# Fewer weight tiles converted during attention, at half the pace, and fewer low-urgency dummy matmuls

## The chip, the cores and the metric

The kernel runs on one core of a Trainium2 chip. The metric is the device time of one execution in microseconds (us). Three runs of the kernel before took 681.79, 682.04 and 682.61 us.

## The reference

The inputs are queries, keys and values (2 batches, 8 heads, 768 positions, head dimension 64, float32), two integers, and five weight matrices in float64. What is computed, in short:

```python
# attention: scores with a slope per head, a local window and a few global keys
scores = q @ k.T / sqrt(64) - slope[h] * dist        # dist: distance, or n_local for a far global key
keep = (key < n_global) | ((rel >= 0) & (rel < n_local))
a = softmax(where(keep, scores, -1e9));  x = a @ v    # then reshaped to 1536 tokens x 512
# first feed-forward layer: h * tanh(softplus(h))
h = x @ w_in;  x = (h * tanh(log1p(exp(min(h, 20))))) @ w_out          # 512 -> 2048 -> 512
# second feed-forward layer: gated
g = x @ w_gate;  out = (g * sigmoid(g) * (x @ w_val)) @ w_out2         # 512 -> 1536 -> 512
```

## The kernel before, in words

The kernel writes its instruction order itself. It first enters every operation of the program in a planner (`Plan`), with the engines that may do it, an estimated cost, what it reads and writes, and a due time. The due time of a TensorE operation is the sum of the TensorE costs entered so far; that of any other operation is 7 us later, unless an operation that needs its result pulls it forward. Then `Plan.order` plays the program through: whenever an engine is free in that play, it takes the ready operation with the earliest due time, wherever in the program it was entered. An operation is ready when its inputs are there and its buffers have come free, in the order in which they were asked for. The resulting order per engine is fixed when the program is built; on the chip each engine works through its list and waits where an input is late.

**Attention** goes over 12 tiles of 128 tokens, each in two steps of four heads (24 steps, variable `s` of the loop). A step has: transposes of queries and keys for the next tile (L440), the score matmuls (L469), the bias and row minimum on DVE (L488), the exponentials on ACT (L322, tile `e`), transposes of the exponentials (L530) and their copies out of the banks (tile `et`). Once per tile the inverse row sums are spread (L501 to L511) and multiplied with the product with the values (L551, L559); the result is split in a high and a low part in tile `x`.

**Feed-forward.** The tokens stand in three chunks of 512. A job is one chunk and one block of 128 hidden columns: 12 matmuls for the hidden block (L362, three passes over high and low parts), the activation on ACT, DVE and POOL, and 12 matmuls for the output. For the first layer jobs go in pairs. A pass is a half of the blocks (8) for one chunk; the output sums over the pass stay in four banks and are copied out where two passes meet. The first pair needs four weight tiles, the first pass sixteen.

**Weight tiles.** A weight tile (a unit, 68 of them) is loaded as float64 (tile `raw`, 512 KB, 2 buffers), turned into float32 by one ACT pass (L393) and four DVE passes (L876 to L879, tile `cv`, 3 buffers), and split into a high part (L345 on ACT or L342 on POOL) and a low part (L353, on POOL or DVE). It ends in one of the 13 buffers `wa`, or, once attention has given up its memory, one of 15 buffers `wb`. The loop over the steps calls `units_to(n)`, which enters conversions until n are entered. The calls behind the loop, between the jobs, enter the others.

**Dummy matmuls.** `warm_up` enters 6 + `LATE` matmuls on a zero tile (L585). The first 6 are due at once. The others are due last of all, so that TensorE takes one when nothing else is ready in the planner's play.

The matmuls of the feed-forward layers get their first banks when the score matmuls are done. The instruction lines in the profile can be lines of helpers (L322, L342, L345, L353, L362); the tile names tell them apart.

Of the kernel before, what the change touches and what calls it, by code (L numbers as in the profile page):

```python
# [212 lines left out]
def kernel(  # L213
# [25 lines left out]
    NWA = 13  # L239
    NWB = 15  # L240
    NST = 2
    WARM = 6
    LATE = 50
    EDGE = 104
    SPARE = 2500.0
    SCALE = -1.0 / float(D) ** 0.5
# [134 lines left out]
    def convert(u):  # L381
        key, (src, view) = units[u]
        raw = plan.buf(raw_p)
        w = plan.buf(cv_p)
        t = plan.buf(w_p)
        where[key] = t
        hi = lambda: raw.t[:, :, 1]
        lo = lambda: raw.t[:, :, 0]
        wf = lambda: w.t.bitcast(F32)
        R, W_ = [(raw, 0)], [(w, 0)]  # L390
        dma(lambda: nc.sync.dma_start(out=view(raw.t), in_=src), [], R, kb=512)
        steps = f64_steps(nc, lambda: w.t, lo, hi)
        op([("A", 520, lambda: nc.scalar.activation(out=wf(), in_=hi().bitcast(F32), func=AF.Abs))], R, W_)  # L393
        for i, fn in enumerate(steps):
            op([("V", (450, 500, 780, 840)[i], fn)], R + W_ if i > 1 else W_, W_)
        copy(lambda: t.t[:, 0], wf, W_, [(t, 0)], on="AG")
        arith(lambda: t.t[:, 1], wf, lambda: t.t[:, 0].bitcast(F32), ALU.subtract, W_ + [(t, 0)], [(t, 1)])
# [6 lines left out]
    def load(i, names="qk"):  # L404
        b, t = tiles[i]
        for nm, src in (("q", q), ("k", k), ("v", v)):
            if nm not in names:
                continue
            x = plan.buf(raw_in[nm])
            raws[nm, i] = x  # L410
            for hs in (slice(0, 4), slice(4, 8)) if i == 0 else (slice(0, H),):
                dma(lambda x=x, src=src, hs=hs: nc.sync.dma_start(
                    out=x.t[:, hs], in_=src[b, hs, t * P:(t + 1) * P, :].rearrange("h s d -> s h d")), [],
                    [(x, hf) for hf in range(hs.start // 4, hs.stop // 4)], kb=32 * (hs.stop - hs.start),
                    prio=-1e6 + hs.start + 9 * (nm == "v") if i == 0 else None)

    def load_previous(i):

        b, t = tiles[i]
        if t == 0:  # L420
            raws["u", i] = raws["v", i]
        elif t < NT - 1:
            x = raws["u", i] = plan.buf(raw_in["u"])
            for ks, k0, hk in ((slice(0, WG), 0, 0), (slice(WG, P), t * P + WG, 1)):
                dma(lambda ks=ks, k0=k0: nc.sync.dma_start(
                    out=x.t[ks], in_=v[b, :, k0:k0 + ks.stop - ks.start, :].rearrange("h s d -> s h d")), [],
                    [(x, hk)], kb=2 * (ks.stop - ks.start))

    def transp(i, hf):
        b, t = tiles[i]  # L430
        xk, xq = raws["k", i], raws["q", i]
        ps = plan.buf(t_p)
        c = t % 2
        prs = slice(2 * hf, 2 * hf + 2)

        def emit():
            for p in range(4):
                x = xq if p % 2 else xk
                h = 4 * hf + p // 2 * 2
                nc.tensor.transpose(ps.t[:, p * P:(p + 1) * P], x.t[:, h:h + 2, :].rearrange("s h d -> s (h d)"), ident)  # L440

        pe(emit, [(xk, hf), (xq, hf)], [(ps, 0)], 4, 128)
        copy(lambda: kq.t[:, prs, c:3:2 - c, :], lambda: ps.t.rearrange("p (a b s) -> p a b s", a=2, b=2), [(ps, 0)],
             [(kq, (c, hf)), (kq, (2, hf))], psum_in=True, on="AV")

    def move_k(i, hf):
        b, t = tiles[i]
        if t == NT - 1:
            return
        prs = slice(2 * hf, 2 * hf + 2)  # L450
        own = lambda: kq.t[:, prs, t % 2, 0:WG]
        g = lambda: kg.t[:, prs, :]
        if t == 0:
            copy(g, own, [(kq, (t % 2, hf))], [(kg, hf)], n=64, on="G")
        else:
            copy(own, g, [(kg, hf)], [(kq, (t % 2, hf))], n=64, on="G")

    def qk(s):
        i, hf = divmod(s, 2)
        b, t = tiles[i]  # L460
        nb = 1 if t == 0 else 2
        banks = scs[s] = [plan.buf(sc_p[0]), plan.buf(sc_p[1])]

        def emit():
            for p in range(2):
                pr = 2 * hf + p
                for j in range(2):
                    ro = slice(64 * j, 64 * j + 64)
                    nc.tensor.matmul(out=banks[j].t[:, p * 256:p * 256 + nb * P], lhsT=kq.t[ro, pr, 2, :],  # L469
                                     rhs=kq.t[ro, pr, 0:nb, :].rearrange("p b s -> p (b s)"), start=True, stop=True)  # L470

        pe(emit, [(kq, (c, hf)) for c in (2, 0, 1)[:nb + 1]], [(banks[0], 0), (banks[1], 0)], 8, 230, "RR")

    def softmax(s):
        i, hf = divmod(s, 2)
        b, t = tiles[i]
        n = P if t == 0 else 2 * P
        banks = scs.pop(s)
        e = ebs[s] = plan.buf(e_p)
        if hf == 0:  # L480
            sms[i] = plan.buf(sm_p)
        sm = sms[i]
        m = lambda u: mn.t[:, s * 4 + u:s * 4 + u + 1]
        for u in range(4):
            p, j = divmod(u, 2)
            h = 4 * hf + u
            bs, c0 = (bias0, 0) if t == 0 else (bias, (1 - t % 2) * P)
            dve(lambda u=u, p=p, j=j, h=h, bs=bs, c0=c0: nc.vector.tensor_tensor_reduce(  # L488
                out=e.t[:, u, 0:n], in0=banks[j].t[:, p * 256:p * 256 + n], in1=bs.t[:, h, c0:c0 + n], scale=SCALE,
                scalar=BIG, op0=ALU.add, op1=ALU.min, accum_out=m(u)),  # L490
                [(banks[j], 0), (bs, h)], [(e, u), (mn, s * 4 + u)], n=n + 8)
        for u in range(4):
            act(lambda u=u: e.t[:, u, 0:n], lambda u=u: e.t[:, u, 0:n], AF.Exp, [(mn, s * 4 + u)],
                [(e, u), (sm, 4 * hf + u)], scale=-1.0, bias_=lambda u=u: m(u),
                accum=lambda u=u: sm.t[:, 4 * hf + u:4 * hf + u + 1], n=n)
# [21 lines left out]
    def turn(s):  # L517

        nb = blocks(s)
        e = ebs.pop(s)  # L520
        ets[s] = []
        for p in range(2):
            ps = plan.buf(t_p)
            et = plan.buf(et_p)
            pv4 = lambda ps=ps: ps.t.rearrange("p (c j s) -> p c j s", c=2, j=2)

            def emit(p=p, pv4=pv4):
                for c in range(nb):
                    for j in range(2):
                        nc.tensor.transpose(pv4()[:, c, j, :], e.t[:, 2 * p + j, c * P:(c + 1) * P], ident)  # L530

            pe(emit, [(e, 2 * p), (e, 2 * p + 1)], [(ps, 0)], 2 * nb, 128)
            copy(lambda et=et: et.t[:, 0:nb], lambda pv4=pv4: pv4()[:, 0:nb], [(ps, 0)], [(et, 0)],
                 psum_in=True, n=256 * nb, on="AV")
            ets[s].append(et)
# [43 lines left out]
    def warm_up(first, later):  # L579
        src, ps = plan.buf(g_p), plan.buf(warm_p)  # L580
        t = lambda: src.t.rearrange("p a c -> p (a c)")
        op([("V", 600, lambda: nc.vector.memset(t()[:, 0:512].bitcast(F32), 0.0))], [], [(src, 0)], prio=-1e5)

        def emit():
            nc.tensor.matmul(out=ps.t, lhsT=t()[:, 0:P], rhs=t()[:, 0:512], start=True, stop=True)  # L585

        for i in range(first + later):
            op([("P", 216, emit)], [(src, 0)], [(ps, i)], prio=-1e5 if i < first else 1e6)
        plan.nominal = 0.0

    def setup():
        warm_up(WARM, LATE)
        load(0, "qk")
# [197 lines left out]
    def units_to(n):  # L791
        while n_units[0] < min(n, len(units), freed[0] + room[0]):
            convert(n_units[0])
            n_units[0] += 1

    NS = 2 * NTL
    for s in range(NS + 2):
        i, hf = divmod(s, 2)
        if s < NS:
            if hf == 0:  # L800
                load_previous(i)
                if i + 1 < NTL:
                    load(i + 1, "v")
            qk(s)
            softmax(s)
            move_k(i, hf)
            if i + 1 < NTL:
                transp(i + 1, hf)
            if hf == 1 and i + 2 < NTL:
                load(i + 2)  # L810
        if 0 <= s - 1 < NS:
            turn(s - 1)
            if s % 2 == 0:
                spread(s // 2 - 1)
                pv(s // 2 - 1)
        units_to(min(NWA, max(0, s - 3)))
        if s == NS:
            flag()
    def switch():
# [299 lines left out]
```

## Time and profile before

| | |
|---|---|
| median of three runs | 682.04 us |
| profiled execution | 681.4 us |
| its span in the profile | 679.6 us |
| granted TensorE clock, mean | 0.996 |
| instructions | 9295 |
| TensorE busy | 660.2 us |
| DVE, ACT, POOL busy | 385.0, 358.6, 273.3 us |

Times in rows are microseconds from the start of the span unless marked ns. PE is TensorE's matmul, PEld its weight load; DVE is VectorE, ACT ScalarE, POOL GpSimd, SP the engine that issues the loads and stores. In a group, "out<-in" names the tiles written and read. Busy time of an engine says that something ran on it, not that it was needed: a dummy matmul counts as busy.

### The profile page before, as it was taken

What the parts mean: (1) busy time and instruction counts of PE and PEld (TensorE: products, weight loads), DVE (VectorE), ACT (ScalarE), POOL (GpSimd) and SP (SyncE); (2) the same over time, 40 slices, a digit from 0 to 9 for tenths busy, and PEclk for the clock granted to TensorE, in tenths of its full rate; (3) what the DMA queues carried; (4) which work ended last, traced back from release to release, by engine and by line L of the source; (5) the groups of instructions that cost most, each with busy time, mean ns of one, the idle gap of its engine ahead of it and who ended that gap; (6) DMA issues with size and microseconds to landing.
All of it is one profiled execution on the core that took longest, in us unless ns stands there. A gap on an engine that the chain in (4) does not pass through costs nothing.

```text
span 679.6 us, 9295 instructions
## 1 busy us (share of the span) xinstructions
PE 660.2 (97%) x3369; PEld 539.4 (79%) x3369; DVE 385.0 (57%) x711; ACT 358.6 (53%) x653; POOL 273.3 (40%) x271
## 2 busy tenths in 40 slices
PE   8999999998998999999989999999999999999996
PEld 5877678887887888888868788888888888888884
DVE  6899978788658475773695798111761121312212
ACT  6999898878775787577758322211521211111110
POOL 3567653754445444563474373211531111111110
PEclk9999999999998999999999999999999999999999
DMA  8788851233334326122043124100300300300301
GB/s 201 187 203 212 216 134 63 92 111 125 98 103 127 110 74 217 62 94 94 31 124 123 63 72 145 62 1 1 123 32 0 124 1 0 124 0 1 125 0 66
DMA packets 80068, 63.58 MB, mean 94 GB/s; under 512 B 48272, under 2 KB 68752, under 8 KB 80016
## 3 DMA queue, kind: packets, MB, share of 16 engines
q1 hardware_dynamic: 80016, 62.93, 30.7%
q8 instruction: 28, 0.46, 0.3%
q14 instruction: 24, 0.20, 0.1%
HBM read 53.48 MB, written 9.44 MB: 93 GB/s over the span
## 4 chain that ended last, share of the span: by engine, by line
PE 72%; ACT 11%; DVE 9%; issue 4%; DMA 2%; POOL 1%; SPq 1%; DVEq 0%; ACTq 0%; POOLq 0%
PE bank L362 62%; PE bank L469 2%; PE bank L530 2%; PE bank L551 2%; ACT u L322 2%; DVE cv L879 2%; ACT e L322 1%; PE bank L585 1%; DVE cv L876 1%; ACT u L698 1%; DVE cv L878 1%; ACT L697 1%; DVE a L353 1%; PE bank L440 1%; ACT cv L393 1%
## 5 line engine op out<-in xcount | busy, mean ns | idle before, releaser
L353 POOL TENSOR_TENSOR g<-a,g 128x512 fp32r<-128x512 f32 x65 | 91.6, 1412 | 228.9 <-ACT g L345 227.8
L362 PE MATMUL bank<-x,wa 128*128 128x512 f32 x756 | 180.0, 390 | 0.0
L362 PEld LDWEIGHTS bank<-x,wa 128*128 128x128 f32 x756 | 141.6, 188 | 29.3
L362 PE MATMUL bank<-x,wb 128*128 128x512 f32 x684 | 162.0, 389 | 0.0
L362 PEld LDWEIGHTS bank<-x,wb 128*128 128x128 f32 x684 | 128.4, 188 | 26.6
L322 ACT ACTIVATE u<-bank 128x512 f32<-128x512 f32 x84 | 49.6, 591 | 119.9 <-PE bank L362 119.7
L716 DVE SCALAR_TENSOR_TENSOR a<-u,bank 128x512 f32<-128x512 f32 x36 | 24.7, 685 | 144.5 <-ACT u L322 144.5
L345 ACT ACTIVATE g<-a 128x512 fp32r<-128x512 f32 x66 | 41.1, 630 | 90.3 <-DVE a L718 78.6
L362 PE MATMUL bank<-g,wa 128*128 128x512 f32 x288 | 71.0, 397 | 3.8 <-DVE st L342 1.9
L362 PE MATMUL bank<-g,wb 128*128 128x512 f32 x288 | 69.1, 389 | 2.6 <-DVE st L577 2.6
L362 PE MATMUL bank<-wa,g 128*128 128x512 f32 x288 | 69.5, 389 | 1.2 <-DVE st L577 1.2
L362 PEld LDWEIGHTS bank<-g,wa 128*128 128x128 f32 x288 | 55.1, 192 | 16.2 <-ACT st L345 2.3
L876 DVE TENSOR_SCALAR cv<-cv 128x512 f32<-128x512 f32 x68 | 43.8, 648 | 41.7 <-ACT cv L393 41.4
L362 PEld LDWEIGHTS bank<-g,wb 128*128 128x128 f32 x288 | 53.9, 188 | 14.2 <-issue 3.0
L362 PEld LDWEIGHTS bank<-wa,g 128*128 128x128 f32 x288 | 54.0, 188 | 12.8 <-ACT cv L393 1.6
L879 DVE SCALAR_TENSOR_TENSOR cv<-raw,cv 128x512 int32<-128x512 int32 x68 | 61.6, 910 | 1.1
L878 DVE SCALAR_TENSOR_TENSOR cv<-raw,cv 128x512 int32<-128x512 int32 x68 | 59.2, 876 | 0.9
L353 POOL TENSOR_TENSOR wa<-cv,wa 128x512 fp32r<-128x512 f32 x32 | 44.5, 1390 | 32.2 <-ACT wa L345 29.8
L353 DVE TENSOR_TENSOR a<-bank,u 128x512 f32<-128x512 f32 x48 | 30.9, 685 | 42.1 <-ACT u L322 41.1
L393 ACT ACTIVATE cv<-raw 128x512 f32<-128x512 f32 x68 | 44.9, 666 | 16.7 <-DMA raw<-in_moe_w_gate_dram 7.5
L353 POOL TENSOR_TENSOR wb<-cv,wb 128x512 fp32r<-128x512 f32 x25 | 36.4, 1459 | 30.0 <-ACT wb L345 29.3
L322 ACT ACTIVATE e<-e,mn 128x256 f32<-128x256 f32 (+1 forms) x96 | 46.0, 487 | 1.7 <-DVE mn L488 1.7
(96 smaller groups left out, 790.8 us busy)
## 6 DMA issues: line engine op xcount, KB each, us to landing
raw<-in_moe_w_out_dram SPq DMA_DIRECT2D x28, 512.0 KB, 3.3
raw<-in_moe_w_in_dram SPq DMA_DIRECT2D x16, 512.0 KB, 3.9
raw<-in_moe_w_gate_dram SPq DMA_DIRECT2D x12, 512.0 KB, 3.5
raw<-in_moe_w_val_dram SPq DMA_DIRECT2D x12, 512.0 KB, 3.5
part<-st SPq DMA_DIRECT2D x12, 256.0 KB, 2.0
part<-sb SPq DMA_DIRECT2D x12, 256.0 KB, 2.2
st<-part SPq DMA_DIRECT2D x12, 256.0 KB, 2.7
sb<-part SPq DMA_DIRECT2D x12, 256.0 KB, 3.7
```

The lines of the kernel that those rows point to most:

```text
L322: nc.scalar.activation(out=o(), in_=i(), func=func, scale=scale, **args)
L345: lambda: nc.scalar.activation(out=o(), in_=i(), func=AF.Copy, scale=scale)),
L353: return lambda: eng.tensor_tensor(out=o(), in0=x(), in1=y(), op=alu)
L362: nc.tensor.matmul(out=o, lhsT=lhs(a), rhs=rhs(b), start=first and i == 0, stop=last and i == len(PASSES) - 1)
L393: op([("A", 520, lambda: nc.scalar.activation(out=wf(), in_=hi().bitcast(F32), func=AF.Abs))], R, W_)
L469: nc.tensor.matmul(out=banks[j].t[:, p * 256:p * 256 + nb * P], lhsT=kq.t[ro, pr, 2, :], rhs=kq.t[ro, pr, 0:nb, :].rearrange("p b s -> p ( ...
L530: nc.tensor.transpose(pv4()[:, c, j, :], e.t[:, 2 * p + j, c * P:(c + 1) * P], ident)
L551: nc.tensor.matmul(out=o.t[64 * j:64 * j + 64, p * P:(p + 1) * P], lhsT=v_of(c).t[:, 2 * p + j, :], rhs=et4[p].t[:, c, j, :], start=c == 0 ...
L716: dve(lambda: nc.vector.scalar_tensor_tensor(out=a.t, in0=u.t[:, 0], scalar=1.0, in1=hg.t, op0=ALU.add, op1=ALU.mult), U + [(hg, 0)], A_)
L876: lambda: ts(out=f(), in0=f(), scalar1=F64_LOW, scalar2=F64_HIGH, op0=ALU.max, op1=ALU.min),
L878: lambda: stt(out=w(), in0=high(), scalar=-0x40000000, in1=w(), op0=ALU.bitwise_and, op1=ALU.bitwise_or),
L879: lambda: stt(out=w(), in0=low(), scalar=29, in1=w(), op0=ALU.logical_shift_right, op1=ALU.bitwise_or),
```

## The change

One constant and one argument change. The loop over the attention steps enters at most nine conversions instead of 13. It enters one for every two steps from step 5 on, instead of one for each step from step 4 on. So the ninth is entered in step 21, where before the thirteenth was entered in step 16. The other four are entered by the calls between the feed-forward jobs, which were there before. The buffers (13 `wa`, 15 `wb`) are as many as before. The dummies that are due last go from 50 to 24.

```diff
-    LATE = 50
+    LATE = 24
...
-        units_to(min(NWA, max(0, s - 3)))
+        units_to(min(9, max(0, (s - 3)//2)))
```

## Rows read from the trace of the kernel before

**Rows 1.** The page, busy time, share of the span, and instructions of each engine.
```profile
PE 660.2 (97%) x3369; PEld 539.4 (79%) x3369; DVE 385.0 (57%) x711; ACT 358.6 (53%) x653; POOL 273.3 (40%) x271
```

**Rows 2.** The page, the chain of waits, shares of the span by engine.
```profile
PE 72%; ACT 11%; DVE 9%; issue 4%; DMA 2%; POOL 1%; SPq 1%; DVEq 0%; ACTq 0%; POOLq 0%
```

**Rows 3.** Windows: length, busy time (instructions) of each engine, granted clock, DMA share, GB/s.
```profile
core 0: us, PE busy (x) PEld busy (x) DVE busy (x) ACT busy (x) POOL busy (x), PEclk, DMA share, GB/s
13.00:29.70 16.70, 16.70 (x150) 13.14 (x150) 13.45 (x52) 16.51 (x55) 7.67 (x15) 1.00 0.78 196
...
29.70:87.90 58.20, 56.08 (x516) 43.73 (x515) 53.99 (x160) 53.94 (x162) 40.95 (x51) 1.00 0.82 211
81.60:101.20 19.60, 18.39 (x175) 14.26 (x174) 14.53 (x57) 18.50 (x57) 12.01 (x17) 1.00 0.64 168
87.90:101.20 13.30, 13.03 (x119) 9.98 (x116) 9.72 (x44) 13.25 (x43) 7.00 (x11) 1.00 0.49 121
101.20:118.60 17.40, 17.40 (x137) 14.46 (x135) 14.30 (x37) 14.14 (x26) 5.75 (x7) 1.00 0.19 61
118.60:165.00 46.40, 46.40 (x207) 38.16 (x205) 37.51 (x52) 36.42 (x46) 29.18 (x24) 1.00 0.32 102
```

**Rows 4.** Groups of PE, dummies of 13 to 29.7 and of 29.7 to 87.9.
```profile
L585 PE MATMUL bank<-g 128*128 128x512 f32 x8 | 3.2, 456 | 0.0
...
L585 PE MATMUL bank<-g 128*128 128x512 f32 x35 | 10.6, 419 | 0.0
```

**Rows 5.** The chain in order of time (start, us, what), longest burst of dummies.
```profile
75.06 1.62 PE bank L585 x7
```

**Rows 6.** Groups of DVE and ACT in 29.7 to 87.9, the conversion's passes.
```profile
L878 DVE SCALAR_TENSOR_TENSOR cv<-raw,cv 128x512 int32<-128x512 int32 x11 | 10.3, 933 | 0.1
L879 DVE SCALAR_TENSOR_TENSOR cv<-raw,cv 128x512 int32<-128x512 int32 x11 | 8.5, 770 | 0.1
L876 DVE TENSOR_SCALAR cv<-cv 128x512 f32<-128x512 f32 x11 | 7.1, 643 | 0.5 <-ACT cv L393 0.5
L877 DVE TENSOR_SCALAR cv<-cv 128x512 int32<-128x512 int32 x10 | 5.7, 572 | 0.0
...
L393 ACT ACTIVATE cv<-raw 128x512 f32<-128x512 f32 x11 | 7.5, 680 | 0.0
```

**Rows 7.** Groups of DVE in 87.9 to 101.2, a pass of the conversion.
```profile
L878 DVE SCALAR_TENSOR_TENSOR cv<-raw,cv 128x512 int32<-128x512 int32 x1 | 0.7, 680 | 0.0
```

**Rows 8.** The page's groups, subtraction that ends a conversion (second pool of tiles).
```profile
L353 POOL TENSOR_TENSOR wb<-cv,wb 128x512 fp32r<-128x512 f32 x25 | 36.4, 1459 | 30.0 <-ACT wb L345 29.3
```

**Rows 9.** The dummies' line in 46 to 101.2: durations, first and last start, form.
```profile
L585 PE MATMUL bank<-g x29: 389/396/502, 45.6 to 81.2; 128*128 128x512 f32 x29
```

**Rows 10.** Timeline of PE (start, us, what), the first feed-forward matmuls behind attention.
```profile
118.58 5.72 PE L362 MATMUL bank<-x,wa 128*128 128x512 f32 x24
124.14 2.88 PE L362 MATMUL bank<-g,wa 128*128 128x512 f32 x12
126.86 2.88 PE L362 MATMUL bank<-x,wa 128*128 128x512 f32 x12
...
132.29 2.88 PE L362 MATMUL bank<-x,wb 128*128 128x512 f32 x12
```

**Rows 11.** Timeline of DVE, a conversion's last pass: units 14 and 15, 18, 24.
```profile
107.56 1.28 DVE L879 SCALAR_TENSOR_TENSOR cv<-raw,cv 128x512 int32<-128x512 int32 x2
...
130.95 0.98 DVE L879 SCALAR_TENSOR_TENSOR cv<-raw,cv 128x512 int32<-128x512 int32 x1
...
159.59 0.69 DVE L879 SCALAR_TENSOR_TENSOR cv<-raw,cv 128x512 int32<-128x512 int32 x1
```

**Rows 12.** Timeline of PE, first matmuls behind two idle times (in brackets).
```profile
166.98 3.04 PE L362 MATMUL bank<-g,wa 128*128 128x512 f32 x12 [1.88 <-ACT st L345]
...
210.02 4.58 PE L362 MATMUL bank<-g,wa 128*128 128x512 f32 x12 [1.89 <-DVE st L342]
```

**Rows 13.** Windows, columns as in rows 3, around the second idle time.
```profile
205.00:216.00 11.00, 9.11 (x33) 7.08 (x32) 8.87 (x13) 7.16 (x9) 5.97 (x5) 0.84 0.57 171
```

## The prediction

> **What bounds the kernel now.** I read the page's table of engines first [rows 1]: TensorE is busy 97% of the span, the next engine 57%. The chain of waits puts only 72% of the span on TensorE, with ACT and DVE next [rows 2], so somewhere the engines that feed it set the pace. The table by stage says where [rows 3]. I cut the span where the kind of work changes: attention before the conversions have set in (13 to 29.7 us), attention with them (29.7 to 87.9), its end with almost none (87.9 to 101.2), the overlap with the first feed-forward jobs (to 118.6), and the first pass over weights (to 165). In 29.7 to 87.9 TensorE looks full (56.08 of 58.20 us), but DVE (53.99) and ACT (53.94) are full too. So the reader must ask what TensorE's time is made of there. The groups of that stretch [rows 4] name 35 dummy matmuls; a burst of seven takes 1.62 us of the chain [rows 5], 0.231 us each. That is 35 x 0.231 = 8.1 us, and 58.20 - 56.08 = 2.1 us are idle: 10.2 of 58.2 us (18%) give nothing to the result, and the work that must be done is 48.0 us. In the stretch before, 8 dummies [rows 4] make 1.8 of 16.70 us, 11%; in the one after, which has no dummy, 0.27 of 13.30 us are idle, 2% [rows 3]. The share follows the conversions: 11 of them fall in the 58.2 us [rows 6], one in the 13.3 us [rows 7].
>
> From 118.6 us on TensorE does feed-forward work nearly without a break (46.40 of 46.40 us to 165 [rows 3]). A microsecond by which attention ends earlier is therefore a microsecond of the total, as long as the weights keep up.
>
> **Part 1: the pace of conversion.** One conversion is four DVE passes and one ACT pass, and then a copy and a subtraction that go to ACT, POOL or DVE. For the 11 of the stretch the four DVE groups sum to 10.3 + 8.5 + 7.1 + 5.7 = 31.6 us and the ACT group is 7.5 us [rows 6]: 39.1 of the 107.9 us that DVE and ACT are busy together. Without conversions the two would need 68.8 us, 34.4 each, if the planner shares the copies out evenly, which their equal busy time says it does. At the old pace they need 54.0 each, more than the 48.0 of TensorE's work: they are the bound. At half the pace they need (68.8 + 19.6) / 2 = 44.2 each, less than 48.0: TensorE's own work becomes the bound, with some waste. The two neighbouring stretches bound that waste: at 2% the 48.0 us take 49.0 us, a gain of 9.2; at 11% they take 53.9, a gain of 4.3. The other end is no gain, if the planner puts the conversions back (second rival). I take 4.7, near the 11%: that stretch has about one and a half conversions in 16.7 us, close to the new pace, and the 2% stretch has no wait for a new tile's inputs left.
>
> **Part 2: four tiles later.** Four conversions leave the limit of the attention loop. They cost DVE 4 x 31.6 / 11 = 11.5 us and must be made between the end of the scores and the first use. DVE is idle 17.40 - 14.30 = 3.1 us in 101.2 to 118.6 and 46.40 - 37.51 = 8.9 us in 118.6 to 165 [rows 3], 12.0 us in all. They fit with nothing to spare. Their cover is that idle time; without it the cost is up to the whole 11.5 us. I cost them at 0.7 us, half of one POOL subtraction of 1459 ns [rows 8], because each must end with one before TensorE may start; bounds 0 and 11.5. Their four 512 KB loads move with them on SP's queue. That queue carries fewer loads while the loads of queries, keys and values run, and a free DMA share of 0.68 or more behind 118.6 us takes them [rows 3]; I count nothing for it.
>
> **Part 3: 26 dummies fewer.** The program keeps 6 + 24 of 56. Of the 56, 29 run after 46 us [rows 9]; the 26 that go are the last of these in the old order. Their whole time is 26 x 0.231 = 6.0 us, but they stand in waits, so by themselves they give back between nothing and 6.0 us. This is the waste that Part 1 already bounds, and I add nothing. What they may cost is the clock. In 81.6 to 101.2 us no dummy runs, TensorE is idle 1.2 us, and the granted clock is 1.00 [rows 3], the 2.4 GHz level. I take no cost; the bound is in the third rival.
>
> **The sum.** -4.7 + 0.7 = -4.0 us. The profiled execution took 681.4 us, of which 679.6 are the span; it lies 0.64 us under the median 682.04. Its sum gives 677.4; the forecast goes by the median: **678.0 us**.
>
> **Rivals.** *Weights come late (slower).* Say that no more than nine tiles are ready when the scores end, 4.7 us sooner than now, at 96.5 us. TensorE then wants the fourth pair's second input tile, the fifteenth unit, at 132.29 - 4.7 = 127.6 us; in the old run it is the first matmul that reads a tile of the second pool [rows 10]. If the order puts 5.4 us of ready output matmuls ahead (24 of them, twice the 2.72 us from 124.14 to 126.86), it can wait until 133.0. Six units must be converted in that time. DVE's last passes show two paces [rows 11]: six units from 131.9 (end of the eighteenth) to 160.3 us (end of the twenty-fourth), 4.7 us each, in which case the last is ready in time; and three, the sixteenth to the eighteenth, in the 23.1 us from 108.8 to 131.9, 7.7 us each. At 6.4, the middle, they end at 96.5 + 38.4 + 2.4 (the copy and the subtraction behind it) = 137.3, and TensorE waits 4.3 us. A wait also costs the clock: behind 1.89 us of idle time twelve matmuls took 4.58 us [rows 12], against 3.04 behind the earlier wait of 1.88 us, and the granted clock of that stretch was 0.84 [rows 13]. With 1.5 for that the stall is 5.8 us. The next point where the passes over the tokens meet (166.98 us [rows 12]) meets the moved conversions too; I put half of its wait of 1.88 us on top, 0.9. The time is 682.0 - 4.7 + 5.8 + 0.9 = 684.0 us. It decides from a pace of about 5.7 us per unit. For it: DVE's idle time is only just enough. Against it: the first four of the six have slots in the first pool and need not wait for the end of attention, as the old ones did.
>
> *The planner makes them all the same (no change).* The limit governs when a conversion is entered in the program, not when it runs. The planner takes any ready operation when an engine is free, and buffers are as many as before. In the old trace two more units than the thirteen asked for pass DVE at 107.56 us, before attention has ended [rows 11]. If idle moments draw in the conversions at the old rate, DVE and ACT remain full and only dummies go: 681.5 us. Against it: such a conversion now ranks behind the attention work that it used to displace.
>
> *The clock falls in attention.* The longest removed burst is 1.62 us [rows 5], close to the 1.89 us behind which the clock fell [rows 12]. Two falls of 1.5 us give 678.0 + 3.0 = 681.0 us. Against it stands the dummy-free stretch at clock 1.00. The Trainium skill, "TensorE: Matmul & The Clock Gate", section "Part 4: PE-mode transpose", says that transposes do not hold the clock up as ordinary matmuls do, and much of attention's TensorE work is transposes; by that rule this rival would be the likely one. The trace does not bear it out in those 19.6 us.
>
> **How the numbers follow.** Forecast 0.56, late weights 0.17, no change 0.20, clock 0.07. About 0.2%, 1.4 us, is what a measurement can tell from no change. The forecast counts as faster, and so do 0.06 of the no-change case (in which some dummies had delayed ready work): 0.62. The rest of it and the clock rival are the same: 0.21. Late weights are slower: 0.17. The forecast's own range is 673.5 (9.2 gained, 0.7 given back) to 680.5. The range of all reaches up over the late-weights case: 673.5 to 685.
>
> **What would show it.** Right: the last score matmuls 3 to 7 us earlier than 99 us, DVE and ACT below 90% busy in the middle of attention, no dummy after some 60 us, clock 1.00, no new idle time of TensorE between 113 and 135 us. Wrong: DVE and ACT as full as before with the same count of conversions by 101 us; a TensorE wait for a weight tile near 128 us; a clock under 1.00 in attention; or waits where passes over the tokens meet (as at 166.98 and 210.02 us [rows 12]) that grow by more than 3 us, since a new order moves what stands on ACT and DVE ahead of the copies out of the banks.

## The result, and the profile after

The changed kernel takes 674.08 us (median of four runs, 671.94 to 674.63) against 681.91 us for the kernel before (681.36 to 682.61): ratio 0.9879 with a 95% interval of 0.9855 to 0.9902. That is 7.8 us or 1.2% less, nearly twice the forecast of 4.0 us. The profiled execution took 674.3 us, with a span of 672.5 us against 679.6.

The page gives the busy time of each engine, and the chain of waits its shares:

```profile
PE 655.7 (97%) x3343; PEld 537.8 (80%) x3343; DVE 386.1 (57%) x717; ACT 355.7 (53%) x647; POOL 272.9 (41%) x271
...
PE 71%; DVE 6%; ACT 5%; issue 3%; POOL 1%; DVEq 0%; ACTq 0%
```

TensorE has 26 instructions fewer, the dummies, and 4.5 us less busy time [rows 1]. ACT's part of the chain has fallen from 11% to 5% [rows 2]. Where the time went stands in the windows of the changed kernel (columns as in [rows 3]; the last two are new places):

```profile
13.00:29.70 16.70, 16.70 (x157) 13.16 (x153) 14.14 (x59) 16.70 (x59) 7.38 (x15) 1.00 0.73 184
29.70:87.90 58.20, 56.43 (x546) 44.53 (x548) 49.78 (x167) 54.57 (x170) 38.46 (x55) 1.00 0.76 193
87.90:101.20 13.30, 13.08 (x118) 10.65 (x115) 12.47 (x48) 12.11 (x38) 6.13 (x8) 1.00 0.39 99
109.00:160.00 51.00, 51.00 (x231) 42.07 (x228) 43.25 (x64) 42.95 (x57) 28.22 (x25) 1.00 0.30 101
200.00:206.00 6.00, 4.80 (x14) 3.84 (x15) 4.02 (x8) 5.72 (x7) 3.44 (x3) 0.72 0.93 300
```

The groups of the changed kernel in 29.7 to 87.9 us (beside [rows 4, 6]):

```profile
L585 PE MATMUL bank<-g 128*128 128x512 f32 x12 | 4.5, 444 | 0.0
...
L878 DVE SCALAR_TENSOR_TENSOR cv<-raw,cv 128x512 int32<-128x512 int32 x8 | 7.6, 952 | 0.1
L879 DVE SCALAR_TENSOR_TENSOR cv<-raw,cv 128x512 int32<-128x512 int32 x8 | 5.9, 732 | 0.0
L876 DVE TENSOR_SCALAR cv<-cv 128x512 f32<-128x512 f32 x7 | 5.4, 769 | 0.5 <-ACT cv L393 0.5
L393 ACT ACTIVATE cv<-raw 128x512 f32<-128x512 f32 x7 | 4.7, 686 | 0.0
L877 DVE TENSOR_SCALAR cv<-cv 128x512 int32<-128x512 int32 x8 | 4.0, 497 | 0.1
```

TensorE's busy time hardly moved (56.08 to 56.43 of 58.20 us), but what it is made of did. Twelve dummies at 0.231 us are 2.8 us, 1.8 us are idle: 4.5 us (8%) give nothing to the result, where it was 10.2 us (18%). Useful work in this stretch rose from 48.0 to 53.7 us. Eight conversions pass DVE instead of 11.

The sources of the dummies (L585), of the score matmuls (L469) and of the matmul that stands right behind attention's last one (L661) say when each starts first and last (first three lines: the changed kernel; last two: the kernel before):

```profile
L585 PE MATMUL bank<-g x30: 390/480/795, 1.5 to 65.7; 128*128 128x512 f32 x30
...
L469 PE MATMUL bank<-kq x192: 272/376/579, 8.0 to 93.5; 64*128 64x256 f32 x160, 64*128 64x128 f32 x32
...
L661 PE MATMUL bank<-ident,chk x1: 270/270/270, 109.2 to 109.2; 128*1 128x128 f32 x1
...
L469 PE MATMUL bank<-kq x192: 272/376/480, 7.0 to 100.1; 64*128 64x256 f32 x160, 64*128 64x128 f32 x32
L661 PE MATMUL bank<-ident,chk x1: 270/270/270, 118.6 to 118.6; 128*1 128x128 f32 x1
```

To compare orders, I cut each span in two. *Attention's end* is the start of the matmul of L661, less 0.2267 us (2.72 us for 12 [rows 10]) for each feed-forward matmul that ran before it. *The rest* is the span behind that start, less 0.2267 us for each of the remaining of 2448 feed-forward matmuls: waits, dummies, matmuls at the lower clock, and the end. Before, L661 starts at 118.6 us with 48 feed-forward matmuls ahead: attention's end 107.7, rest 17.0. After, 109.2 with 36 ahead: 101.0 and 16.6. In these two profiles 6.7 us came from attention and 0.4 us from behind it, 7.1 us of the two spans; the medians are 0.7 us further apart.

Behind attention the changed kernel has two TensorE waits of 0.15 us or more:

```profile
201.20 4.58 PE L362 MATMUL bank<-g,wa 128*128 128x512 f32 x12 [1.92 <-DVE st L342]
...
337.71 4.58 PE L362 MATMUL bank<-g,wb 128*128 128x512 f32 x12 [4.05 <-DVE st L577]
```

The kernel before has four there: the two of [rows 12], one of 2.60 and one of 1.17 us, 7.5 us in all. The first two have become one, the last two another; together they are 6.0 us.

### The profile page after: what moved, and what is told of

Read it like the earlier page. It is cut to its first block, busy times and chain, and to the rows that moved or that the text cites. A ratio compares the mean times of both kernels' runs of the same rounds, so it can differ in the third digit from the quotient of the medians.

```text
span 672.5 us, 9245 instructions
## 1 busy us (share of the span) xinstructions
PE 655.7 (97%) x3343; PEld 537.8 (80%) x3343; DVE 386.1 (57%) x717; ACT 355.7 (53%) x647; POOL 272.9 (41%) x271
## 4 chain that ended last, share of the span: by engine, by line
PE 71%; DVE 6%; ACT 5%; issue 3%; POOL 1%; DVEq 0%; ACTq 0%
PE bank L362 70%; ACT u L322 2%; DVE cv L879 2%; DVE cv L878 1%; DVE a L353 1%; ACT u L698 1%; ACT L697 1%; ACT L699 1%; DVE cv L876 1%; ACT cv L393 1%; PE bank L551 1%; ACT wb L345 0%; DVE g L353 0%; DVE cv L877 0%; PE bank L530 0%
## 5 line engine op out<-in xcount | busy, mean ns | idle before, releaser
L353 POOL TENSOR_TENSOR g<-a,g 128x512 fp32r<-128x512 f32 x63 | 89.2, 1419 | 235.8 <-ACT g L345 234.7
L345 ACT ACTIVATE g<-a 128x512 fp32r<-128x512 f32 x70 | 43.4, 631 | 90.5 <-DVE a L718 81.8
L362 PE MATMUL bank<-g,wb 128*128 128x512 f32 x288 | 70.7, 396 | 4.0 <-DVE st L577 4.0
L876 DVE TENSOR_SCALAR cv<-cv 128x512 f32<-128x512 f32 x68 | 45.7, 675 | 44.0 <-ACT cv L393 44.0
L362 PEld LDWEIGHTS bank<-g,wb 128*128 128x128 f32 x288 | 55.0, 192 | 16.2 <-issue 4.4
L879 DVE SCALAR_TENSOR_TENSOR cv<-raw,cv 128x512 int32<-128x512 int32 x68 | 63.3, 935 | 1.1
L878 DVE SCALAR_TENSOR_TENSOR cv<-raw,cv 128x512 int32<-128x512 int32 x68 | 57.4, 849 | 0.8
L353 DVE TENSOR_TENSOR a<-bank,u 128x512 f32<-128x512 f32 x48 | 31.0, 685 | 30.9 <-ACT u L322 29.7
L877 DVE TENSOR_SCALAR cv<-cv 128x512 int32<-128x512 int32 x68 | 46.8, 691 | 1.1
```

The source lines that it names most:

```text
L345: lambda: nc.scalar.activation(out=o(), in_=i(), func=AF.Copy, scale=scale)),
L353: return lambda: eng.tensor_tensor(out=o(), in0=x(), in1=y(), op=alu)
L362: nc.tensor.matmul(out=o, lhsT=lhs(a), rhs=rhs(b), start=first and i == 0, stop=last and i == len(PASSES) - 1)
L876: lambda: ts(out=f(), in0=f(), scalar1=F64_LOW, scalar2=F64_HIGH, op0=ALU.max, op1=ALU.min),
L877: lambda: ts(out=w(), in0=w(), scalar1=3, scalar2=0x3FFFFFF8, op0=ALU.logical_shift_left, op1=ALU.bitwise_and),
L878: lambda: stt(out=w(), in0=high(), scalar=-0x40000000, in1=w(), op0=ALU.bitwise_and, op1=ALU.bitwise_or),
```

## The experiments

The rows *before* and *after* are the runs of the result. All others were timed in five rounds beside the kernel before, in five sets on five chips; its medians there lay between 681.6 and 682.7 us. Across sets the ratios compare best. The table gives the runs by the two changed arguments ("loop" is the argument of `units_to`, `h` stands for `(s - 3)//2`); attention's end and rest are of the profiled execution.

| run | loop | late dummies | us | ratio [95%] | end | rest |
|---|---|---|---|---|---|---|
| before | 13, s-3 | 50 | 681.9 | 1 | 107.7 | 17.0 |
| after | 9, h | 24 | 674.08 | 0.9879 [0.9855, 0.9902] | 101.0 | 16.6 |
| after_again | 9, h | 24 | 675.01 | 0.9885 [0.9856, 0.9914] | 100.1 | 15.5 |
| e1 | 13, s-3 | 24 | 682.98 | 1.0018 [0.9999, 1.0037] | 111.3 | 14.6 |
| e2 | 9, h | 50 | 678.51 | 0.9945 [0.9928, 0.9963] | 99.2 | 22.5 |
| e3 | as before, last 26 not emitted | 24 | 681.53 | 0.9996 [0.9980, 1.0011] | 108.3 | 17.3 |
| e4 | 9, s-3 | 50 | 681.89 | 0.9998 [0.9983, 1.0012] | 108.2 | 16.2 |
| g1 | as e2, last 20 not emitted | 30 | 677.98 | 0.9935 [0.9911, 0.9958] | 99.3 | 22.3 |
| f1 | 9, h | 0 | 677.66 | 0.9926 [0.9899, 0.9953] | 102.5 | 18.6 |
| f2 | none | 24 | 675.67 | 0.9903 [0.9874, 0.9932] | 102.0 | 16.7 |
| i1 | 9, h; sums on ACT | 50 | 685.66 | 1.0056 [1.0033, 1.0079] | 99.2 | 29.8 |
| i2 | 9, h; sums on ACT | 24 | 680.53 | 0.9963 [0.9943, 0.9984] | 100.7 | 23.1 |
| h1 | 9, s-3 | 24 | 678.89 | 0.9953 [0.9935, 0.9970] | 108.7 | 16.6 |
| h2 | 13, h | 24 | 673.76 | 0.9873 [0.9836, 0.9911] | 101.2 | 17.0 |
| h3 | 6, (s-3)//3 | 24 | 675.75 | 0.9914 [0.9899, 0.9929] | 101.5 | 17.4 |
| k28 | 9, h | 28 | 673.88 | 0.9867 [0.9832, 0.9902] | 101.3 | 17.1 |
| k40 | 9, h | 40 | 677.55 | 0.9934 [0.9910, 0.9958] | 98.9 | 20.9 |
| m1 | 9, h; banks first | 24 | 674.25 | 0.9880 [0.9856, 0.9905] | 100.8 | 18.1 |
| m2 | 9, h; banks first | 50 | 677.56 | 0.9941 [0.9917, 0.9965] | 100.0 | 20.8 |
| m3 | 13, s-3; banks first | 50 | 682.64 | 1.0004 [0.9981, 1.0028] | 108.1 | 15.5 |

Several of these kernels have the same order of work. Engine by engine, the traces of after_again, h2 and m1 list the same instructions in the same sequence as *after*, and m2 as e2, m3 as *before*; e3 and g1 have the sequence of *before* and e2 without the dummies that were left out. f2 and h3 differ by one exchange of two neighbouring passes. So these rows are repeats, and they say how far two profiles of one order lie apart: the new order ends attention at 100.1 to 101.2 us with a rest of 15.5 to 18.1, the old one (with e3 and m3) at 107.7 to 108.3 with 15.5 to 17.3. By them attention gains 6.5 to 8.2 us, and a difference of the rests cannot be told.

### One part at a time

**e1: 24 dummies alone.**

```diff
-    LATE = 50
+    LATE = 24
```

> The dummy half of the change alone: 24 instead of 50, with the order planned anew, conversions as before. Theory A: 680 to 682.5, the 13 conversions still fill DVE and ACT. Theory B: 675 to 677.5, the gain of the whole change less one or two us.

**e2: the new conversions alone.**

```diff
-        units_to(min(NWA, max(0, s - 3)))
+        units_to(min(9, max(0, (s - 3)//2)))
```

> The conversion half of the change alone: nine at half the pace, 50 dummies. Theory A: 674 to 677, last score matmuls at 93 to 95 us, and the dummies that are left over run in gaps that exist. Theory B: the 26 dummies stay in the order and cost their 6.0 us: 679.5 to 682.

**e3: the order of before kept, the last 26 dummies not emitted.**

```diff
-            op([("P", 216, emit)], [(src, 0)], [(ps, i)], prio=-1e5 if i < first else 1e6)
+            op([("P", 216, emit if i < 30 else lambda: None)], [(src, 0)], [(ps, i)], prio=-1e5 if i < first else 1e6)
```

> The kernel before with its order of work kept on every engine; only the last 26 of the 56 dummy matmuls are not issued. Theory A (the pace of conversion keeps DVE and ACT full, the dummies stand in waits that would be there anyway): 26 x 0.231 = 6.0 us of dummies turn into idle time of TensorE, the time stays within 1.5 us of before, 680.5 to 682.5. Theory B (the dummies themselves hold up work that is ready): TensorE gets back most of the 6.0 us, 675.5 to 677.5. If the clock needs the dummies: a granted clock under 1.00 between 46 and 101 us and a time over 683.

**e4: nine tiles at the old pace, 50 dummies.**

```diff
-        units_to(min(NWA, max(0, s - 3)))
+        units_to(min(9, max(0, s - 3)))
```

> The limit of nine conversions alone, entered one per step as before, 50 dummies. Theory A: the pace is the old one until step 12, so only the last third of attention gains, 1 to 2.5 us: 679 to 681. Theory B: no gain or a loss, 681 to 683.

e3 and e1 are worth nothing within their intervals, as Theory A had it (e1 lies 0.5 us above its range). In e3 TensorE idles where dummies stood. Its last dummy starts at 47.2 us; the window behind it, in the kernel before and then in e3:

```profile
47.70:101.20 53.50, 51.12 (x466) 39.22 (x465) 46.98 (x153) 50.53 (x155) 34.42 (x46) 1.00 0.73 188
...
47.70:101.20 53.50, 47.02 (x442) 35.15 (x443) 48.14 (x153) 50.83 (x156) 35.06 (x48) 1.00 0.77 194
```

And two stretches of attention in e1:

```profile
29.70:87.90 58.20, 51.26 (x464) 38.91 (x464) 54.57 (x156) 52.47 (x158) 45.06 (x56) 0.97 0.81 203
87.90:101.20 13.30, 13.09 (x124) 10.65 (x123) 10.49 (x37) 11.51 (x39) 6.03 (x9) 0.87 0.54 146
```

In e3 TensorE's busy time fell by 4.1 us, attention's end moved by 0.6, and the clock stayed at 1.00 over 53.5 us without a dummy. So the 26 stood in waits. e4 shows that the number nine by itself does nothing either. e2 is the part that speeds attention up, by 8.5 us; but 5.5 us are lost again behind attention, and 3.0 us of the spans are left (3.5 of the medians), between the ranges of both theories. The two parts alone are worth -3.5 and +0.9 us, together -7.8: they are not a sum.

### What the larger number of dummies costs once attention is shorter

In e2 the dummies that found no wait in attention come in one block right behind it, and the first pass over the weights ends with a wait (timeline of TensorE, then of DVE before that wait):

```profile
107.39 3.00 PE L362 MATMUL bank<-x,wa 128*128 128x512 f32 x12
110.23 4.70 PE L585 MATMUL bank<-g 128*128 128x512 f32 x20
114.76 2.88 PE L362 MATMUL bank<-x,wa 128*128 128x512 f32 x12
...
161.17 4.58 PE L362 MATMUL bank<-g,wa 128*128 128x512 f32 x12 [2.73 <-DVE st L342]
```

```profile
158.79 1.63 DVE L879 SCALAR_TENSOR_TENSOR cv<-raw,cv 128x512 int32<-128x512 int32 x1
160.34 1.28 DVE L342 TENSOR_SCALAR st<-bank 128x512 f32<-128x512 f32 x2
```

The copies of the output sums (tile `st`) free the banks for the next pass; here they stand on DVE behind conversion passes. Either the block costs its 4.5 us, or the order with its waits does. g1 keeps e2's order and leaves the block out (its 20 dummies are not issued):

```diff
-            op([("P", 216, emit)], [(src, 0)], [(ps, i)], prio=-1e5 if i < first else 1e6)
+            op([("P", 216, emit if i < 36 else lambda: None)], [(src, 0)], [(ps, i)], prio=-1e5 if i < first else 1e6)
...
-        units_to(min(NWA, max(0, s - 3)))
+        units_to(min(9, max(0, (s - 3)//2)))
```

> The kernel with the conversion half alone (nine at half the pace, 50 dummies), order of work kept; only its last 20 dummies, which run as one block from 110.23 to 114.76 us behind the attention, are not issued. Theory C (with a faster attention the unused dummies end up in a wait that the planner expects and that is not there; they hold up ready feed-forward matmuls by 4.5 us): 673.5 to 675. Theory D (the wait is there, a weight tile or a bank is late, and the changed kernel gains its extra 4.5 us by another order): 678 to 679, with 3 to 4.5 us of idle time in place of the block.

The result is e2's, 677.98 us: nothing came back, as Theory D had it. TensorE starts the pair 4.5 us sooner and waits for the same copies later. The timeline of TensorE in g1, then its window and DVE's copy:

```profile
127.26 0.73 PE L362 MATMUL bank<-x,wb 128*128 128x512 f32 x2 [0.45 <-POOL wb L342]
128.62 2.57 PE L362 MATMUL bank<-x,wb 128*128 128x512 f32 x10 [0.62 <-POOL wb L353]
...
160.07 5.46 PE L362 MATMUL bank<-g,wa 128*128 128x512 f32 x12 [4.41 <-DVE st L342]
```

```profile
155.00:166.00 11.00, 6.59 (x17) 4.91 (x17) 9.82 (x14) 8.00 (x10) 5.32 (x5) 0.69 0.58 191
```

```profile
159.25 1.27 DVE L342 TENSOR_SCALAR st<-bank 128x512 f32<-128x512 f32 x2
```

The copies start 1.1 us sooner than in e2 (159.25 against 160.34), not 4.5 us; the two waits for weight tiles near 128 us are those of the first rival, 1.1 us in all. The wait takes up 1.7 us more, and twelve matmuls behind it take 5.46 instead of 4.58 us. Behind attention TensorE's waits of 0.15 us or more are 6.4 us in e2, 9.0 in g1 and 6.0 in the changed kernel. So what e2 loses it loses in its block, but without the block its order waits as long instead: the order is the price, not the dummies' own time. In the changed kernel the same copies are on ACT, in time (timeline of ACT, then TensorE, which goes on without a wait):

```profile
157.51 1.09 ACT L345 ACTIVATE st<-bank 128x512 f32<-128x512 f32 x2
```

```profile
158.30 2.90 PE L362 MATMUL bank<-g,wa 128*128 128x512 f32 x12
```

The changed kernel was run again in the same set, unaltered, beside one with no late dummy (`LATE = 0`) and one in which the loop enters nothing (`units_to(0)`).

> The changed kernel itself, beside the others on one chip: 672 to 676 by both theories.

> The changed kernel with no late dummies at all (6 instead of 30 in all). Theory C and the first one (dummies inside attention stand in waits): 673 to 675, as the changed kernel, because 24 x 0.231 = 5.5 us turn into idle time. Theory D' (dummies delay ready work inside attention too): 669 to 671. If the clock needs them: granted clock under 1.00 before 100 us and over 676.

> The changed kernel with no conversion entered by the attention loop (24 late dummies): all are entered behind the first feed-forward jobs and run in attention only where the planner finds an engine free. Theory of the pace: attention ends earlier still, last score matmuls at 88 to 92 us, and the weights come late: waits of TensorE for weight tiles between 100 and 140 us of 5 us or more, 676 to 684 in all. Rival (the planner fills every idle moment with conversions wherever they are entered): at least nine conversions done by 95 us, 672 to 676.

f1 is not faster but 2.7 to 3.6 us slower than the two runs of the changed kernel, outside the ranges of its theories; so what halving the dummies brings is not the TensorE time of dummies. f2 keeps attention's end at 102.0, as the rival said: conversions that are entered only behind the loop still fill idle moments of the play, and ten have passed DVE by 100 us, as many as in the changed kernel.

### Forcing the copies of the sums

If those copies on DVE are the cause, allowing them on ACT alone should mend e2 (i1) and leave the changed kernel as it is (i2):

```diff
-                copy(lambda st=st: st.t, lambda y=y: y.t, Y, T, scale=1.0 if kind == 1 else 0.5, psum_in=True, on="AV")
+                copy(lambda st=st: st.t, lambda y=y: y.t, Y, T, scale=1.0 if kind == 1 else 0.5, psum_in=True, on="A")
```

> The conversion half alone (50 dummies) with one more edit: the partial sums of a pass leave their banks on ACT only, no longer on ACT or DVE as the planner likes. Theory E (what the conversion half loses again is lost where the first pass ends, because the copies of the sums stand on DVE behind conversions: 2.73 us of wait and 1.6 us of lower clock): no wait over 0.6 us where the first pass ends, 673 to 676. Rival (the block of 20 dummies costs by itself): 677 to 679 with the wait gone.

> The changed kernel with the same edit (partial sums leave on ACT only). Theory E: the wait of 1.92 us where the second pass ends goes, with the lower clock behind it, 1.5 to 3.5 us less than the changed kernel: 671 to 673.5. Rival (ACT's chain of tables and logarithms holds the copies up as long): 674 to 677.

Theory E missed in both. Both are slower, by some 7 and 6 us against e2 and the changed kernel. The page of waits of i1 (us in total, times, longest) shows why:

```profile
PE bank L362 <- ACT st L345: 7.7, 3, 2.9
PE bank L362 <- DVE st L577: 4.3, 3, 1.7
```

The wait moves to ACT, where the copies now stand behind activations, and comes at three meetings of passes; in e2 the wait for the copies comes at one, with 2.7 us, and that for the additions (L577) is 3.7 us. The other way to have them sooner is a due time 1000 ns earlier for the operations that free the banks (the copy and two additions on DVE), with the changed kernel (m1), with e2 (m2) and with the kernel before (m3):

```diff
-                copy(..., psum_in=True, on="AV")
+                copy(..., psum_in=True, on="AV").prio = plan.nominal - 1000.0
...
-                dve(lambda st=st, y=y: tt(st.t, y.t, st.t, ALU.add), Y, T)
+                dve(lambda st=st, y=y: tt(st.t, y.t, st.t, ALU.add), Y, T).prio = plan.nominal - 1000.0
```

> The changed kernel; the operations that take the sums out of the banks at the end of a pass get a due time 1 us before that of the matmuls entered so far, in place of 7 us behind it. Theory F (the waits where passes end come from this late due time): the waits of 1.92 and 4.05 us shrink to under 1 us each and the lower clock behind them goes, 3 to 7 us less: 667 to 672. If the waits have another cause: 673 to 676.

> The conversion half alone with 50 dummies and the same early due time. Theory F: it loses its waits where passes end too and keeps only the block of 20 dummies, so it stands at most 4.5 us above the kernel before it in this list, 669 to 675. If the number of dummies costs by itself: the block's 4.5 us on top, 673 to 677. If neither: 677 to 680.

> The kernel before (13 conversions at full pace, 50 dummies) with the same early due time. Theory F: its waits of 1.88, 1.89, 2.60 and 1.17 us shrink, 3 to 8 us less: 674 to 679; its attention still ends 6 to 8 us later than that of the changed kernel.

None differs from its counterpart by more than 1 us, and the traces say why: the edit moved no instruction on any engine. So m1, m2 and m3 are repeats. They neither bear out nor refute that earlier copies would mend the waits; they show that this due time is not what places the copies.

The traces show something else there. The program counts 450, 500, 780 and 840 ns for the four DVE passes of a conversion. The six passes in front of the copies are 4.2 us by that count. In e2 they took 6.6 us (153.87 to 160.42) and TensorE waited 2.73; in the changed kernel, in front of its wait at 201.20 us, 5.5 (194.99 to 200.45) and 1.92. So it can be that the play has DVE free for the copies in time, and the chip has not. No run tested this; why the passes take longer stands in the last section.

### Pace or number, and how many dummies

h1 takes the old pace with the new number, h2 the new pace with the old limit (which the loop does not reach: it ends at 11), h3 an even lower pace; k28 and k40 change the dummies only.

```diff
-        units_to(min(9, max(0, (s - 3)//2)))
+        units_to(min(9, max(0, s - 3)))            # h1
+        units_to(min(NWA, max(0, (s - 3)//2)))     # h2
+        units_to(min(6, max(0, (s - 3)//3)))       # h3
...
-    LATE = 24
+    LATE = 28                                      # k28
+    LATE = 40                                      # k40
```

> The changed kernel with its cap of nine and 24 late dummies, but one conversion entered per step as before. If the pace makes the gain: last score matmuls at 97 us or later, as with 50 dummies (98.0), and 679 to 683. If the number of nine makes it: last score matmuls at 92 to 95 us, 673 to 677.

> The changed kernel with its pace but without the cap of nine (the loop reaches 11), 24 late dummies. If the pace, that is the due times of the conversions, makes the gain and not their number: last score matmuls at 92 to 95 us and 673 to 677. If the number makes it: part of the gain goes, last score matmuls at 96 us or later, 677 to 680.

> The changed kernel with six conversions entered, one per three steps. If the pace makes the gain and half is enough to make TensorE the bound of attention: last score matmuls at 91 to 95 us as in the changed kernel, 672 to 677. If attention still waits for DVE and ACT at half the pace: last score matmuls at 88 to 91 us. Weights that come late would show as a wait of TensorE for a weight tile between 105 and 140 us.

> The changed kernel with 28 late dummies instead of 24: a neutral edit that only makes the planner play another order. If the dummies matter by their time: 4 x 0.231 = 0.9 us at most, 674 to 676. If the order behind attention is what differs between plans: attention ends as before within 1.5 us, and the waits where passes end differ by up to 5 us, 673 to 679.

> The changed kernel with 40 late dummies. If left-over dummies behind attention cost their time: a block of about 10 there, 2.3 us, 675.5 to 678. If only the order decides: anything from 673 to 679, with the difference in the waits where passes end.

Sorted by attention's end, the table falls in two: every order at the old pace (before, e1, e3, e4, h1, m3) ends attention at 107.7 to 111.3 us, every order at half of it or less at 98.9 to 102.5, with whatever limit and whatever dummies. With nine conversions in both, and the same dummies, h1 against the changed kernel and e4 against e2 differ by the pace alone: 108.7 against 101.0 (h1 with some time at the lower clock, see below), and 108.2 against 99.2 (neither with any in attention). So the later entry makes the gain in attention, not the number. h2 adds nothing to this, since its two further entries, in steps 23 and 25, moved no instruction.

What the later entry does is less clear than the prediction had it. The stretch of attention in f2, and in it the instructions that write or read the tile `cv`, in the kernel before, in e4 and in f2 (here the busy times are those of DVE, ACT and POOL):

```profile
29.70:87.90 58.20, 56.03 (x541) 44.20 (x537) 54.85 (x170) 54.51 (x171) 37.98 (x54) 1.00 0.76 187
```

```profile
29.70:87.90 58.20, 33.84 (x46) 9.97 (x15) 16.21 (x15) 1.00 0.82 211
...
29.70:87.90 58.20, 28.81 (x38) 7.37 (x11) 15.43 (x15) 1.00 0.79 200
...
29.70:87.90 58.20, 27.86 (x34) 5.39 (x8) 13.51 (x14) 1.00 0.76 187
```

In f2 DVE and ACT are as full as before [rows 3], and their conversions take 33.3 us of the two, against 36.2 in e4; yet attention ends 6.2 us sooner. From the kernel before to e4 the same sum falls from 43.8 to 36.2 us, and attention ends no sooner. So neither how full the two engines are nor the time that conversions take there sorts the orders; the pace of entry does. That points to the rank of a conversion among the ready operations. No run shows it by itself, since none changed the rank and kept the conversions.

With 40 dummies the block behind attention is there again, with ten of them, and the rest is 20.9:

```profile
110.00 2.43 PE L585 MATMUL bank<-g 128*128 128x512 f32 x10
```

With 24 or 28 there is none. k28, another order, equals the changed kernel within its interval; no version tried beats it clearly.

h1 also shows the third rival's mechanism. Its stretch of attention, and three cuts of it:

```profile
29.70:87.90 58.20, 53.27 (x478) 41.08 (x478) 51.10 (x161) 52.18 (x160) 39.91 (x52) 0.94 0.78 196
60.00:65.00 5.00, 4.58 (x40) 3.19 (x36) 4.21 (x15) 4.41 (x15) 3.99 (x7) 1.00 0.75 184
65.00:70.00 5.00, 3.10 (x16) 1.98 (x16) 5.00 (x16) 3.95 (x13) 3.86 (x4) 0.75 1.03 267
70.00:75.00 5.00, 5.00 (x34) 3.87 (x30) 2.11 (x9) 2.50 (x10) 3.02 (x6) 0.57 0.04 10
```

TensorE idled 1.9 of the 5 us in 65 to 70, in waits for copies of `et` and a product on DVE, and the granted clock was 0.57 in the 5 us behind. Both orders that were planned anew at the old pace with 24 dummies (e1, h1) show such a fall; no order at half pace was seen to.

## Why the prediction was right or wrong

- **Part 1, the pace: the term was mis-sized; this is the step that failed.** It was to gain 4.7 us, from a waste near 11%. The gain measured is 6.7 us (6.5 to 8.2 over the repeats; in e2, 8.5), and the waste 8%: by the same arithmetic 48.0 / 0.922 = 52.0 us, a gain of 6.2. I had leaned on a stretch before the conversions in full pace; that stretch itself held three dummies fewer after the change. The two bounds (4.3 and 9.2) held.
- **How Part 1 got there: not as described.** Half the pace was to be half the conversions, with DVE and ACT at 44.2 us each, less than TensorE's 48.0. Eight conversions ran in 58.2 us, 73% of the old number, since the planner draws in others, as the second rival said. By the prediction's own sum that is (68.8 + 28.4) / 2 = 48.6 each, which does not make TensorE the bound. DVE fell to 86% busy, as foreseen; ACT, foreseen under 90%, stayed at 94%; in f2 and h3 both stay as full as before, and attention is 5.7 to 6.2 us shorter all the same. What holds is that the later entry shortens attention, and that dummies and the number of tiles do not (e1, e3, e4, h1). That the gain fell between bounds drawn from the load was in part luck.
- **Part 2, four tiles later: 0.7 us of cost was not seen.** TensorE is busy in all 51.00 us from 109 to 160. The rest is 0.4 us shorter in the first two profiles, but two profiles of one order differ by more than 0.7, so the term was too small to be told. With Part 1's 2.0 us these 1.1 make up the 3.1 us between the forecast 4.0 and the 7.1 of the spans.
- **Part 3, dummies: right alone, wrong in company.** By themselves they give nothing back (e3, e1). I had not seen that a shorter attention has no waits for 50 of them, and that the planner then makes another, worse order behind attention: 3.5 to 4.4 us between e2 and the two runs of the changed kernel.
- **The rivals.** Late weights: no such wait in the changed kernel; in g1, with TensorE 4.5 us sooner, 1.1 us of it came near 128 us as described. (The pace of 6.4 us in that rival is called the middle of 4.7 and 7.7; the middle is 6.2, and its stall 1.2 us less.) All made the same: false by the time, half true by the counts. The clock: 1.00 throughout attention, so false here; where it fell in attention, in h1, idle time came first. In e3 transposes and other matmuls, mixed, ran without a dummy at 1.00. The Trainium skill, "TensorE: Matmul & The Clock Gate", section "Part 4: PE-mode transpose", says that transposes do not hold the clock up. The stretch of e3 does not bear that out, and as a mixture it does not refute it.
- **The signs named.** The last score matmul came 6.6 us earlier, at 93.5 us (foreseen 3 to 7; it had stood at 100.1, not 99), the last dummy at 65.7 us (foreseen some 60); TensorE has no new idle time between 113 and 135 us. The late wait at 337.71 us is 1.5 us longer than its counterpart of 2.60 us before, inside the 3 us named.

**Open.** Whether a lower load or the later rank of the conversions shortens attention (the runs point to the rank). And what in the planner's play, between 24 or 28 dummies and 40 or 50, decides whether the copies of the sums stand on ACT or behind conversions on DVE. g1 shows that the order matters and not the block; i1 and i2 show that ACT alone does not mend it. The rest ranges from 14.6 to 29.8 us among these orders, against 15.5 to 18.1 for that of the changed kernel.

## What to carry to other kernels

Where filler stands in the waits of the engine that looks full, count it as waste, and ask what makes it wait: taking the filler out gave nothing here, entering the competing work later did. Time parts of a change together as well as alone, since a list scheduler answers each edit with a new order everywhere behind it. When an engine comes sooner to a point where a later copy frees its buffers, the time saved is lost there, unless the copy comes sooner too. And before the time of an edited plan is read, compare the orders: m1, m2, m3 and h2 moved nothing, and their times are repeats.

## What the runs showed of the hardware

Two executions of the same program, with the same wait, went on at different speeds. The changed kernel's second profile has the wait of 201.20 us here:

```profile
200.34 3.00 PE L362 MATMUL bank<-g,wa 128*128 128x512 f32 x12 [1.93 <-DVE st L342]
```

Twelve matmuls took 3.00 us behind 1.93 us of idle time; in the first profile 4.58 behind 1.92, with a granted clock of 0.72 in 200 to 206 us. So behind an idle time of this length the 1.2 GHz level comes in some executions only, and costs 1.6 us when it does.

And a conversion pass of one form takes 0.7 us or up to 1.8. The trace says when. In e2 (timeline of DVE, then of POOL):

```profile
155.91 1.78 DVE L879 SCALAR_TENSOR_TENSOR cv<-raw,cv 128x512 int32<-128x512 int32 x1
157.61 0.41 DVE L877 TENSOR_SCALAR cv<-cv 128x512 int32<-128x512 int32 x1
158.06 0.70 DVE L878 SCALAR_TENSOR_TENSOR cv<-raw,cv 128x512 int32<-128x512 int32 x1
158.79 1.63 DVE L879 SCALAR_TENSOR_TENSOR cv<-raw,cv 128x512 int32<-128x512 int32 x1
```

```profile
154.19 2.94 POOL L353 TENSOR_TENSOR g<-a,g 128x512 fp32r<-128x512 f32 x2 [3.63 <-ACT g L345]
158.43 1.44 POOL L353 TENSOR_TENSOR wb<-cv,wb 128x512 fp32r<-128x512 f32 x1 [1.30 <-ACT wb L345]
```

The two long passes start while a POOL instruction runs and end 0.55 us behind its end (157.13 and 159.87); the pass at 158.06 was under way when POOL's began, and took 0.70. In the changed kernel all 24 passes of L878 and L879 over 1.2 us started so and ended 0.54 to 0.56 us behind POOL's instruction, and those under 0.75 us started with no POOL instruction running, in the last 0.2 us of one, or within 0.01 us of its start. So by this timing POOL's work lengthens DVE's, though POOL is busy only 41% of the span.
